# Local attention outputs of batches 3 to 7: probabilities as weights, and the rows turned by two DMA transposes a batch

## The chip, the cores and the metric

The kernel runs on one core of a Trainium2 chip. The metric is the device time of one execution in microseconds (us). A core has TensorE (PE, matrix multiplies, with its weight loads shown apart as PEld), VectorE (DVE), ScalarE (ACT), GpSimd (POOL) and SyncE (SP), each with an instruction queue of its own that is worked in order, and 16 DMA engines that all queues' transfers share. In this kernel SP asks for most transfers out of SBUF, and POOL for the loads, which turn f32 into bf16 on the way.

## The reference

Eight batches of causal sparse attention with eight heads (576 positions of 64) are followed by a feed-forward stage with a bilinear product. Heads 0 to 3 are local (a window of 32 positions), heads 4 to 7 strided (positions that agree modulo 32).

```python
scores = scale * np.matmul(q, k.transpose(0, 1, 3, 2))
rel = pos[:, None] - pos[None, :]
mask_local = (rel >= 0) & (rel < stride)
mask_strided = (rel >= 0) & (pos[None, :] % stride == pos[:, None] % stride)
scores = np.where(masks[None, :, :, :], scores, -1000000000.0)
attn = np.exp(scores - np.max(scores, axis=-1, keepdims=True))
attn = attn / (np.sum(attn, axis=-1, keepdims=True) + 1e-09)
attn_out = np.matmul(attn, v)
...
x = attn_out.transpose(0, 2, 1, 3).reshape(B * S, H * D)    # 4608 x 512
out = ((x @ w_a) * (x @ w_b)) @ w_out                        # d_ff = 1536
```

## The kernel before

**Two streams in one order.** The instruction order of each engine is written out by hand. The backbone is the feed-forward stage: nine tiles t of 512 tokens, each with 12 slots `ffn_ab` (f = 0 to 11; eight matmuls at L581, four with `wa_sb` and four with `wb_sb`, 512 tokens moving) and then four slots of the output product (`ffn_ys` at L669 for tiles 2 to 7, `ffn_y` at L733 for tiles 0 and 1; the last tile is written by `y_tail`). Slots are numbered through: 16 t + f. Attention is woven in: `take(i)` runs the steps of the table `LATER` for slot i and `IN_Y` for points within the output product. For batches b from 3 on, positions count from 16 (b - 1), so batch b is made during tile b - 1, and tile b needs it: `xT` holds the feed-forward's input with features on partitions, four chunks c of 128 features (c = 0 and 1 local heads, c = 2 and 3 strided heads) by a ring of 4 x 576 tokens. Tile t = b starts at token 512 b, batch b at token 576 b, and a matmul covers all 512 tokens of the tile (in tile 4 it is cut in two where the ring wraps). The first slot of a tile (f = 0) takes chunk 3 last, chunk 1 last in tile 1.

**A step S** (`S_p`, `S_x`, `S_m`) makes the scores of a unit u (chunk c = u // 2, half = u % 2), their exponentials (L392, ScalarE) and applies the mask in place (L402, VectorE). Keys lie on partitions, queries along the row: `p` is [keys, 2 heads, 288 queries]. Units 0 to 3 are local, with G = 3 blocks of 96 queries, and 4 to 7 strided, with 4 blocks of 72.

**A step V** makes the outputs of a unit. There are two forms:
- `step_VT` (batches 2 to 7): the values are the weights and p moves, 96 columns a block (L485, six matmuls for a local unit). The values' tile has columns of ones behind its 64 columns (`VW` = 128, set by `fill_v`), so the result `o` has 64 rows of outputs, already with features on partitions, and 64 rows of equal sums. The reciprocal is made on ScalarE as exp(-ln) (L494, L495, 64x576 each), and VectorE multiplies into `xT`, once for each head (L499 local, L501 strided).
- `V_p`, `V_r`, `V_n` (batches 0 and 1): p is the weights and the values move, 65 columns a block (64 and one of ones; L441). The result has queries on partitions; VectorE makes the reciprocals (L449) and multiplies into a row tile `xr` (L464). The steps X of TensorE (L510) then turn the rows, and ScalarE copies them into `xT` (L522).

Both forms have one PSUM buffer `o` from tile 0's end on.

**SP's queue.** A step D (`step_D`) transposes parts of q and k in 32x32 blocks on VectorE, and after the last part SP asks for the moves of the blocks into `kT` and `qz`: two moves for k's first pairs of heads, and ten after q's last part (L341, L345). In tile b - 1 the steps D of batch b + 1 run: its local k at slots 3 and 5, its local q at 7 and 9, its strided parts at 12 to 17. At one slot, `take` comes ahead of the steps D. `store_half` (L664) of the tile before is at slots 2 and 3. POOL's loads (L202, L211, L224, L242) each follow a `pace` instruction that reads something of their slot.

Of the kernel before, what the change touches and what calls it, by code (L numbers as in the profile page):

```python
# [8 lines left out]
BF16 = mybir.dt.bfloat16  # L9
# [5 lines left out]
FIRST_D = 2  # L15
RL = 6
RS = 8
# [4 lines left out]
LW = 96  # L22
# [8 lines left out]
def kernel(  # L31
# [10 lines left out]
    nc = tc.nc  # L42
    B, H, S, D = q.shape
# [9 lines left out]
    HL = H // 2  # L53
# [5 lines left out]
    sb = ctx.enter_context(tc.tile_pool(name="sb", bufs=3))  # L59
    fsb = ctx.enter_context(tc.tile_pool(name="ffn", bufs=2))  # L60
    pst = ctx.enter_context(tc.tile_pool(name="pst", bufs=1, space=bass.MemoryType.PSUM))
    dram = ctx.enter_context(tc.tile_pool(name="dram", bufs=2, space=bass.MemoryType.DRAM))
# [19 lines left out]
    vl_buf = [const.tile([128, HL * 6, VW], BF16, name=f"vl{i}") for i in range(2)]  # L82
# [30 lines left out]
    def zero_qz(i, eng, parts=((0, 0), (0, 1), (1, 0), (1, 1))):  # L113
        for j, z in parts:
            t = qz_buf[i][j][z]
            if (i, j, z) == (0, 0, 0):
                t = t[:, 1]
            if eng is nc.scalar:
                nc.scalar.copy(t, spare[:, :1].unsqueeze(2).to_broadcast(list(t.shape)))
            else:  # L120
                eng.memset(t, 0.0)
# [36 lines left out]
    XR = 4  # L158
    xT = const.tile([128, KD, XR * S], BF16)
# [11 lines left out]
    def fast_w(n, gs):  # L171
        a, b = ((wov[:, 0, 1], wov[:, 0, 0]), (wov[:, 1, 1], wf[:, 0]), (wov[:, 1, 1], wov[:, 0, 1]),
                (wov[:, 1, 0], wf[:, 1]))[n]
        nc.vector.tensor_tensor(wf[:, n, gs], a[:, gs], b[:, gs], op=ALU.subtract)
# [3 lines left out]
    def blocks(nm, z):  # L178
        z = int(z)
        return sb.tile([128, 2, (S, RS * GP)[z]], BF16, tag=f"t{nm}{z}", name=f"t{nm}{z}", bufs=1)  # L180
# [84 lines left out]
    def by_row(t):  # L265
        return t.rearrange("p (r h d) -> p h r d", h=2, d=D)

    def pair_up(nm, c):

        if (nm, c) == ("k", 1):  # L270
            t = shared[1][:96, -RL * 128:]
        else:
            t = blocks(*{"k0": "q0", "q0": "q1", "q1": "k0"}[f"{nm}{c}"])
            t = t.rearrange("p h n -> p (h n)")[:96, :RL * 128]
        nc.vector.tensor_copy(by_row(t), nats[1, nm, False][:, 2 * c:2 * c + 2])
        paired[1, nm, c] = t.rearrange("p (r m) -> p r m", r=RL)
# [85 lines left out]
    def unit(u):  # L362

        c, half = u // 2, u % 2
        return (c, half, 128, LW, 3) if c < 2 else (c, half, NP, NP, 4)
# [46 lines left out]
    xn = {}  # L412

    def V_p(b, u):
        c, half, M, n, G = unit(u)
        p = ps.pop((b, u))
        if b == 0:

            o = psum4["o"].tile([128, 512], F32, tag="o", name="o")
            if c < 2:  # L420
                of = o[:, :2 * G * (D + 1)].rearrange("p (j g e) -> p j g e", j=2, e=D + 1)
                sm = of[:, :, :, D:]
            else:
                of = o.rearrange("p (j g e) -> p j g e", j=2, e=D)
                sm = psum4["sum"].tile([128, 2, 4, 1], F32, tag="sum", name="sum")
        else:
            o = psum4["o"].tile([128, 2, 512], F32, tag="o", name="o")
            of = o[:, :, :G * (D + 1)].rearrange("p j (g e) -> p j g e", e=D + 1)
            sm = of[:, :, :, D:]
        for i in range(G):  # L430
            for j in range(2):
                if c < 2:
                    vt = vl_buf[b % 2][:, (2 * c + j) * 6 + 3 * half + i, 0:D + 1]
                elif b == 0:
                    r = 2 * i + j
                    vt = nats[0, "v", c - 2][:NP, half, r * D:(r + 1) * D]
                else:
                    vt = vs_buf[b % 2][:, 2 * (c - 2) + half, 2 * i + j, 0:D + 1]
                w = vt.shape[1]
                pt = p[:M, j, i * n:i * n + 128]  # L440
                nc.tensor.matmul(of[:, j, i, :w], lhsT=pt, rhs=vt, start=True, stop=True)  # L441
                if b == 0 and c >= 2:
                    nc.tensor.matmul(sm[:, j, i], lhsT=pt, rhs=vl_buf[0][:M, 0, D:D + 1], start=True, stop=True)
        held[b, "o", u] = of[:n, :, :, :D], sm[:n]

    def V_r(b, u):
        c, half, M, n, G = unit(u)
        rc = sb.tile([128, 2, 4], F32, tag="rc", name="rc")
        nc.vector.reciprocal(rc[:n, :, :G].unsqueeze(3), held[b, "o", u][1])  # L449
        held[b, "rc", u] = rc  # L450

    def V_n(b, u):
        c, half, M, n, G = unit(u)
        ov, _ = held.pop((b, "o", u))
        rc = held.pop((b, "rc", u))
        if (b, c // 2) not in xn:
            x = sb.tile([128, RS * 4 * D], BF16, tag="xr", name="xr", bufs=2)
            xn[b, c // 2] = x[:n, :S // n * 4 * D].rearrange("p (g h d) -> p g h d", h=4, d=D)
        x = xn[b, c // 2][:, :, 2 * (c % 2):2 * (c % 2) + 2, :]
        if c < 2 or b >= FIRST_D:  # L460
            dst = x[:, G * half:G * half + G].rearrange("p g j d -> p j g d")
        else:
            dst = x[:, :, half, :].rearrange("p (g j) d -> p j g d", j=2)
        nc.vector.tensor_mul(dst, ov, rc[:n, :, :G].unsqueeze(3).to_broadcast([n, 2, G, D]))  # L464

    def step_V(b, u):
        if b >= FIRST_D:
            step_VT(b, u)
            return
        V_p(b, u)  # L470
        V_r(b, u)
        V_n(b, u)

    def step_VT(b, u):

        c, half, M, n, G = unit(u)
        p = ps.pop((b, u))
        o = psum4["o"].tile([128, 2, 512], F32, tag="o", name="o")
        for i in range(G):
            for j in range(2):  # L480
                if c < 2:
                    vt = vl_buf[b % 2][:, (2 * c + j) * 6 + 3 * half + i]
                else:
                    vt = vs_buf[b % 2][:, 2 * (c - 2) + j, 4 * half + i]
                nc.tensor.matmul(o[:, j, i * n:(i + 1) * n], lhsT=vt, rhs=p[:M, j, i * n:(i + 1) * n], start=True, stop=True)  # L485

        r = sb.tile([128, RS * 4 * D], BF16, tag="xr", name="xr", bufs=2)[:64, :4 * W].bitcast(F32)
        r = r.rearrange("p (j w) -> p j w", j=2)
        if c < 2:
            sums = o[64:, :, :W]  # L490
        else:

            sums, r = (t.rearrange(e, p=NP) for t, e in ((o[64:, :, :W], "d j (g p) -> d j p g"), (r, "d j (p g) -> d j p g")))
        nc.scalar.activation(r, sums, ACT.Ln)  # L494
        nc.scalar.activation(r, r, ACT.Exp, scale=-1.0)  # L495
        for j in range(2):
            dst = xT[64 * j:64 * j + 64, c, S * (b % XR):S * (b % XR + 1)]
            if c < 2:
                nc.vector.tensor_mul(dst[:, W * half:W * (half + 1)], o[:64, j, :W], r[:, j])  # L499
            else:  # L500
                nc.vector.tensor_mul(dst.rearrange("d (p r) -> d p r", r=RS)[:, :, G * half:G * (half + 1)],  # L501
                                     o[:64, j, :W].rearrange("d (g p) -> d p g", p=NP), r[:, j])
# [21 lines left out]
    def step_X(b, c):  # L524
# [20 lines left out]
    LATER = {-1: "S0", 0: "S1", 1: "V0", 2: "S2", 3: "V1", 4: "S3", 5: "V2", 6: "S4", 7: "V3", 8: "S5", 9: "V4", 10: "S6",  # L545
             11: "V5"}
    IN_Y = {2: "S7", 6: "V6", 11: "V7"}
    FN = {"Tk": step_Tk, "Tq": step_Tq, "S": step_S, "V": step_V, "X": step_X, "W": lambda b, n: fast_w(n, slice(0, 3)),
          "s": S_px, "m": S_m, "L": lead_vl, "Pk": lambda b, c: pair_up("k", c), "Pq": lambda b, c: pair_up("q", c),
          "Z": lambda b, n: zero_qz(0, nc.vector, ((1, 1),)), "D": lambda b, n: step_D(FIRST_D, 0, "k", n)}  # L550

    def run(b, slot):
# [209 lines left out]
    with tc.manual_schedule(engines={ENG.PE, ENG.SP, ENG.Pool, ENG.DVE, ENG.Activation}):  # L762
# [11 lines left out]
        for x, src in ((raw[0], k), (raw[1], q)):  # L774
            nc.sync.dma_start(out=x[:96].rearrange("p (h r d) -> p h r d", h=2, d=D),
                              in_=src[0, 0:2].rearrange("h (p r) d -> p h r d", r=RL))
# [62 lines left out]
        for b in range(1, B):  # L839
            for pos, names in (STEPS.get(b) or {16 * (b - 1) + x: n for x, n in LATER.items()}).items():  # L840
                steps.setdefault(pos, []).append((b, names.split()))
# [6 lines left out]
        def do(i, fn, *args):  # L848
            at.setdefault(i, []).append(lambda: fn(*args))
# [34 lines left out]
        for i, jz in ((2, (0, 0)), (3, (1, 0)), (0, (0, 1))):  # L884
            do(i, zero_qz, 0, nc.vector, (jz,))
        do(14, rezero, 1)
        do(27, fill_v, vl_buf[1])
        do(28, fill_v, vs_buf[1])
        for n, slot in enumerate((16, 16, 19, 20)):
            do(slot, fast_w, n, slice(3, 6))  # L890
# [50 lines left out]
```

## Time and profile before

| what | before |
|---|---|
| median of 3 runs | 328.92 us (328.76 to 329.47) |
| profiled execution, whole | 329.03 us |
| its span, in which the profile counts | 327.3 us |
| tiles 2, 3, 4, 5, 6 of the feed-forward stage, about | 34.0, 34.0, 34.6, 34.0, 33.8 us |
| share of the chain of waits: L581 / L669 / L733 | 54% / 17% / 6% |
| share of the chain of waits: L485 / L441 | 4% / 1% |
| granted TensorE clock, mean | 0.998 |

A tile is about 34 us, and an `ffn_ab` slot without attention work in it about 1.73 us of TensorE. The chain of waits goes back from the last instruction to what released each, so its shares add to the span; busy times of engines overlap and don't. In the lists of groups, the number ahead of the second bar is the mean of one instruction in ns; what stands behind that bar is idle time of the engine ahead of the group. In the order of time, an engine's lines give start, length and the group; matmuls follow each other closer than their length, so two starts tell the distance.

### The profile page before, as it was taken

What the parts mean: (1) busy time and instruction counts of PE and PEld (TensorE: products, weight loads), DVE (VectorE), ACT (ScalarE), POOL (GpSimd) and SP (SyncE); (2) the same over time, 40 slices, a digit from 0 to 9 for tenths busy, and PEclk for the clock granted to TensorE, in tenths of its full rate; (3) what the DMA queues carried; (4) which work ended last, traced back from release to release, by engine and by line L of the source; (5) the groups of instructions that cost most, each with busy time, mean ns of one, the idle gap of its engine ahead of it and who ended that gap; (6) DMA issues with size and microseconds to landing.
All of it is one profiled execution on the core that took longest, in us unless ns stands there. A gap on an engine that the chain in (4) does not pass through costs nothing.

```text
span 327.3 us, 7626 instructions
## 1 busy us (share of the span) xinstructions
PE 319.6 (98%) x2788; PEld 205.5 (63%) x2820; DVE 250.6 (77%) x529; ACT 210.1 (64%) x345; POOL 151.6 (46%) x280
## 2 busy tenths in 40 slices
PE   8999999999999999999999999999999999999994
PEld 6754555455555587557999885569555954584474
DVE  6766788888778989799879988998878745626652
ACT  6763775478777776777677767876777743323341
POOL 8935948599966554664475346644011001100000
PEclk9999999999999999999999999999999999999999
DMA  9999999999999699999899969897033040004004
GB/s 154 151 203 201 202 184 174 174 173 127 140 213 120 87 95 84 98 222 100 80 85 199 127 69 99 175 159 84 20 78 114 2 131 0 0 2 129 0 2 128
DMA packets 98725, 37.50 MB, mean 115 GB/s; under 512 B 76672, under 2 KB 95744, under 8 KB 98688
## 3 DMA queue, kind: packets, MB, share of 16 engines
q0 software_dynamic: 85968, 19.48, 64.4%
q1 hardware_dynamic: 12576, 17.47, 18.3%
q8 instruction: 22, 0.36, 0.4%
q14 instruction: 15, 0.12, 0.1%
q10 hardware_dynamic: 144, 0.07, 0.1%
HBM read 39.51 MB, written 9.44 MB: 150 GB/s over the span
## 4 chain that ended last, share of the span: by engine, by line
PE 90%; POOL 3%; DMA 3%; DVE 1%; issue 1%; ACT 0%; POOLq 0%
PE mm L581 54%; PE mm L669 17%; PE mm L733 6%; PE st L384 4%; PE o L485 4%; DMA wb_sb<-in_moe_w_b_dram 3%; PE mm L698 2%; POOL shared L196 1%; PE end L698 1%; POOL vl L224 1%; PE o L441 1%; POOL wa_sb L251 0%; POOL tk L237 0%; PE tp L286 0%; PE tp L295 0%
## 5 line engine op out<-in xcount | busy, mean ns | idle before, releaser
L581 PE MATMUL mm<-xT,wb_sb 128*128 128x512 bf16 (+1 forms) x465 | 109.1, 357 | 0.3
L581 PE MATMUL mm<-xT,wa_sb 128*128 128x512 bf16 (+1 forms) x451 | 107.7, 356 | 1.1
L598 ACT COPY a_sb<-mm 128x512 f32<-128x512 f32 x106 | 62.1, 586 | 45.7 <-PE mm L581 45.0
L907 POOL CAST pace<-pf 1x1 f32<-1x1 bf16 x87 | 24.6, 283 | 113.0 <-DVE pf L601 109.8
L581 PEld LDWEIGHTS <-wb_sb 128*128 128x128 bf16 x480 | 46.2, 98 | 44.7 <-DMA wb_sb<-in_moe_w_b_dram 1.1
L601 DVE TENSOR_TENSOR pf<-a_sb,mm 128x512 bf16<-128x512 f32 x84 | 57.0, 679 | 18.5 <-PE mm L581 14.2
L581 PEld LDWEIGHTS <-wa_sb 128*128 128x128 bf16 x480 | 42.7, 98 | 31.3
L494 ACT ACTIVATE xr<-o 64x576 f32<-64x576 f32 x48 | 31.1, 648 | 22.8 <-PE o L485 22.5
L392 ACT ACTIVATE p<-st 128x576 bf16<-128x576 f32 (+1 forms) x64 | 41.6, 650 | 6.3 <-PE st L384 5.7
L495 ACT ACTIVATE xr<-xr 64x576 f32<-64x576 f32 x48 | 32.8, 683 | 1.5
L499 DVE TENSOR_TENSOR xT<-o,xr 64x288 bf16<-64x288 f32 x48 | 21.6, 449 | 13.5 <-ACT xr L495 13.0
L501 DVE TENSOR_TENSOR xT<-o,xr 64x288 bf16<-64x288 f32 x48 | 21.4, 446 | 11.8 <-ACT xr L495 11.2
L669 PEld LDWEIGHTS <-ps 128*128 128x128 bf16 x288 | 27.9, 98 | 3.1
L646 ACT COPY y_sb<-mm 128x512 f32<-128x512 f32 (+1 forms) x28 | 15.6, 556 | 17.9 <-PE mm L669 13.0
L669 PE MATMUL mm<-wf,ps 128*128 128x256 bf16 x216 | 25.6, 273 | 0.0
L733 PE MATMUL mm<-wo_sb,pf 128*128 128x512 bf16 x93 | 22.9, 379 | 0.1
L242 POOL DMA_DIRECT2D vs<-in_v_dram x24 | 19.7, 820 | 5.0 <-PE mm L669 2.4
L669 PEld LDWEIGHTS <-pf 128*128 128x128 bf16 x216 | 20.3, 98 | 2.5 <-issue 0.2
L669 PE MATMUL mm<-wo_sb,pf 128*128 128x256 bf16 x144 | 18.5, 273 | 0.1
L603 DVE TENSOR_TENSOR pf<-a_sb,mm 128x512 bf16<-128x512 f32 x22 | 14.9, 677 | 4.7 <-ACT a_sb L598 2.6
L211 POOL DMA_DIRECT2D ql<-in_q_dram x24 | 16.0, 666 | 5.0 <-DMA wo_sb<-in_moe_w_out_dram 3.9
L211 POOL DMA_DIRECT2D kl<-in_k_dram x24 | 16.0, 667 | 4.8 <-issue 4.0
(152 smaller groups left out, 471.6 us busy)
## 6 DMA issues: line engine op xcount, KB each, us to landing
out_dram<-y_sb SPq DMA_DIRECT2D x12, 512.0 KB, 4.9
out_dram<-y_sb SPq DMA_DIRECT2D x11, 256.0 KB, 3.8
vl<-in_v_dram POOLq DMA_DIRECT2D x6, 384.0 KB, 6.8
kl<-in_k_dram POOLq DMA_DIRECT2D x24, 72.0 KB, 3.4
ql<-in_q_dram POOLq DMA_DIRECT2D x24, 72.0 KB, 3.3
vs<-in_v_dram POOLq DMA_DIRECT2D x24, 72.0 KB, 3.7
wo_sb<-in_moe_w_out_dram POOLq DMA_DIRECT2D x4, 384.0 KB, 9.0
natk<-in_k_dram POOLq DMA_DIRECT2D x20, 72.0 KB, 3.3
```

The lines of the kernel that those rows point to most:

```text
L211: nc.gpsimd.dma_start(out=t[32 * h:32 * h + 32], in_=src[b, h].rearrange("(i y) d -> y i d", y=32))
L392: nc.scalar.activation(p[:M, :, :W], st[:M, :, :W], ACT.Exp, scale=scale)
L494: nc.scalar.activation(r, sums, ACT.Ln)
L495: nc.scalar.activation(r, r, ACT.Exp, scale=-1.0)
L499: nc.vector.tensor_mul(dst[:, W * half:W * (half + 1)], o[:64, j, :W], r[:, j])
L501: nc.vector.tensor_mul(dst.rearrange("d (p r) -> d p r", r=RS)[:, :, G * half:G * (half + 1)], o[:64, j, :W].rearrange("d (g p) -> d p g", ...
L581: nc.tensor.matmul(ps_[:, c0:c0 + n], lhsT=w[:, kk, 128 * f:128 * (f + 1)], rhs=xT[:, kk, x0:x0 + n], start=(kk == first and c0 == 0), sto ...
L598: nc.scalar.copy(a_sb, ab[0])
L601: nc.vector.tensor_mul(pf[:, f, :].rearrange("p (i a s) -> p a i s", i=2, s=16), halves(a_sb), halves(ab[1]))
L669: nc.tensor.matmul(bank[b][:, q], lhsT=lhs(g, q), rhs=rhs(g), start=k in "172" and q == 0 and g == 0, stop=g == FG - 1, skip_group_check=True)
L733: nc.tensor.matmul(ybank[j], lhsT=pf[:, f, 128 * j:128 * (j + 1)], rhs=wo_sb[:, f], start=(f == 0), stop=(f == FD - 1))
L907: nc.gpsimd.tensor_copy(pace, done)
```

## The change

For batches 3 to 7 the local units (u = 0 to 3) take the second form: `step_V` goes to `step_VT` only for strided units and for batch 2. The rows of a batch's four local units are gathered in a tile `xl` (96 queries of a block on partitions, 6 blocks, 256 features). After V3, at slot 7, a new step O asks SP to write them to a buffer in DRAM (576 rows of 256 features; two buffers in turn). At slot 10 a new step I asks SP, for chunk 0 and for chunk 1, for a DMA transpose of 128 features of all 576 rows into `xT`. The steps D at slot 9 come before it, so on SP's queue the write stands between the moves of slot 5 and those of slot 9, and the two transposes behind the ten moves of slot 9 and ahead of those of slot 14. For batch 7, which has no steps D in its tile, the transposes directly follow the write. The steps X are not used for these rows. The fill of the ones in the second local values' buffer (`vl_buf[1]`, at slot 27) falls away; the column that the sums need is set elsewhere (L104).

```diff
@@ V_n
         if (b, c // 2) not in xn:
-            x = sb.tile([128, RS * 4 * D], BF16, tag="xr", name="xr", bufs=2)
+            if b >= FIRST_D:
+                x = sb.tile([128, RL * 4 * D], BF16, tag="xl", name="xl", bufs=1)
+            else:
+                x = sb.tile([128, RS * 4 * D], BF16, tag="xr", name="xr", bufs=2)
...
     def step_V(b, u):
-        if b >= FIRST_D:
+        if b >= FIRST_D and (u >= 4 or b == FIRST_D):
             step_VT(b, u)
             return
...
+    scratch = {}
+
+    def rows_out(b, _):
+
+        scratch[b] = dram.tile([S, HL * D], BF16, tag="xd", name="xd")
+        nc.sync.dma_start(out=scratch[b].rearrange("(g p) e -> p g e", p=LW),
+                          in_=xn.pop((b, 0)).rearrange("p g h d -> p g (h d)"))
+
+    def rows_in(b, c):
+
+        nc.sync.dma_start(out=xT[:, c, S * (b % XR):S * (b % XR + 1)], in_=scratch[b][:, 128 * c:128 * (c + 1)],
+                          transpose=True)
...
     LATER = {-1: "S0", 0: "S1", 1: "V0", 2: "S2", 3: "V1", 4: "S3", 5: "V2", 6: "S4",
-             7: "V3", 8: "S5", 9: "V4", 10: "S6", 11: "V5"}
+             7: "V3 O0", 8: "S5", 9: "V4", 10: "S6 I0 I1", 11: "V5"}
...
+          "O": rows_out, "I": rows_in,
...
-        do(27, fill_v, vl_buf[1])
```

More of the change, by code (lines that the diff above doesn't have):

```diff
@@ L544 @@
                  27.5: "V4", 28: "S6", 28.5: "V5", 29: "S7", 29.5: "V6", 30.5: "V7"}}
-    LATER = {-1: "S0", 0: "S1", 1: "V0", 2: "S2", 3: "V1", 4: "S3", 5: "V2", 6: "S4", 7: "V3", 8: "S5", 9: "V4", 10: "S6",
+    LATER = {-1: "S0", 0: "S1", 1: "V0", 2: "S2", 3: "V1", 4: "S3", 5: "V2", 6: "S4", 7: "V3 O0", 8: "S5", 9: "V4", 10: "S6 I0 I1",
              11: "V5"}
@@ L548 @@
     FN = {"Tk": step_Tk, "Tq": step_Tq, "S": step_S, "V": step_V, "X": step_X, "W": lambda b, n: fast_w(n, slice(0, 3)),
-          "s": S_px, "m": S_m, "L": lead_vl, "Pk": lambda b, c: pair_up("k", c), "Pq": lambda b, c: pair_up("q", c),
+          "s": S_px, "m": S_m, "L": lead_vl, "O": rows_out, "I": rows_in, "Pk": lambda b, c: pair_up("k", c), "Pq": lambda b, c: pair_up("q", c),
           "Z": lambda b, n: zero_qz(0, nc.vector, ((1, 1),)), "D": lambda b, n: step_D(FIRST_D, 0, "k", n)}
```

## The prediction

> **What bounds the kernel now.** I read the page's busy shares first, then its chain of waits, then the stages, then the order of time on TensorE and on SP's queue around one tile boundary.
>
> ```profile
> span 327.3 us, 7626 instructions
> PE 319.6 (98%) x2788; PEld 205.5 (63%) x2820; DVE 250.6 (77%) x529; ACT 210.1 (64%) x345; POOL 151.6 (46%) x280
> PE 90%; POOL 3%; DMA 3%; DVE 1%; issue 1%; ACT 0%; POOLq 0%
> ```
>
> TensorE is on 90% of the chain. Since matmuls overlap, busy time alone proves little, so I look at when each group starts:
>
> ```profile
> 53.69 0.35 PE L441 MATMUL o<-vl,p 128*128 128x65 bf16 x6
> 53.88 0.42 PE L510 MATMUL tp<-ident,xr 96*128 96x96 bf16 x6
> ...
> 207.03 0.42 PE L485 MATMUL o<-p,vl 128*128 128x96 bf16 x6
> 207.28 1.03 PE L581 MATMUL mm<-xT,wa_sb 128*128 128x512 bf16 x4
> ```
>
> The first column is a group's start. The next group starts 0.25 us after an old local unit (L485, 96 columns moving) and 0.19 us after a unit of the new form, which batch 1 already runs (L441, 65 columns; the other free-standing ones give 0.19 and 0.18). TensorE's whole list of waits holds 1.5 us, all before 57 us. So from 93 to 263 us, where batches 3 to 7 are made, TensorE sets the time: what it is spared comes off, and what it is made to wait comes on.
>
> Then the end of tile 5 (its outputs of batch 6 are read by tile 6), on SP's queue and on TensorE:
>
> ```profile
> 218.57 0.55 SPq L345 DMA_DIRECT2D qz10l<-tq  x1
> ...
> 224.25 0.59 SPq L345 DMA_DIRECT2D qz11l<-tq  x1
> 229.16 1.14 SPq L341 DMA_DIRECT2D kT1s<-tk  x2
> ```
> ```profile
> 229.38 0.21 PE L384 MATMUL st<-qz11l,kT1l 128*128 128x96 bf16 x1
> 229.63 0.59 PE L581 MATMUL mm<-xT,wa_sb 128*128 128x512 bf16 x2
> ```
>
> Ten moves keep SP's queue from 218.57 to 224.84 (some 0.63 apart), and the next tile's first L581 is due at 229.42 (the six L384 start 0.042 apart; of the eight first L581 one record is missing). That is the room for what is asked for behind the moves.
>
> **The change, part by part.**
>
> *TensorE.* 20 units (4 local units in each of 5 batches) go from 0.25 to 0.185 us: 20 x 0.065 = 1.3 us saved. Bounds: by columns alone, 6 x (96 - 65) x (0.25/576) = 0.081 a unit, 1.6 in all; nothing, if loading the masked weights p were no longer covered. I take 1.3, since batch 1's row has this very instruction with this very weight load. The weights now wait for the mask on VectorE, but S runs two or three slots ahead of its V, and each slot is 2 us.
>
> *ScalarE and VectorE.*
>
> ```profile
> L494 ACT ACTIVATE xr<-o 64x576 f32<-64x576 f32 x48 | 31.1, 648 | 22.8 <-PE o L485 22.5
> L495 ACT ACTIVATE xr<-xr 64x576 f32<-64x576 f32 x48 | 32.8, 683 | 1.5
> L499 DVE TENSOR_TENSOR xT<-o,xr 64x288 bf16<-64x288 f32 x48 | 21.6, 449 | 13.5 <-ACT xr L495 13.0
> L464 DVE TENSOR_TENSOR xr<-o,rc 96x384 bf16<-96x384 f32 x8 | 4.3, 547 | 0.2
> L449 DVE RECIPROCAL rc<-o 96x6 f32<-96x6 f32 x8 | 1.5, 188 | 2.4 <-PE o L441 2.2
> ```
>
> The shares behind the second bar are idle time. A unit drops L494 and L495 (1.331 us of ScalarE, 26.6 in all) and changes two L499 (0.898) for L449 and L464 (0.735): 3.3 us less VectorE. Both lie beside TensorE, so I cost them at nothing. The single o bank is freed sooner. One stall on VectorE stands in the chain, at tile 4's first output matmul (185.18, some 0.5 us late), but it follows strided unit V4 and its exponentials, which stay; it is a bound below (-0.5). The dropped fill of vl (1.4 us of POOL) is beside everything too.
>
> *SP's queue: three issues a batch.* Rows out: V3 is at slot 7, and in tile 5 its last VectorE instruction ends near 213.6 (it takes the place of the L499 of 212.84, 0.735 long). SP is then held by two k moves until 214.31, so it writes from 214.3 to 214.9, and the q moves behind it, which VectorE lets go at 218.57, are not delayed. The nearest writes to DRAM (256 to 512 KB) land in 3.8 to 4.9 us, so these 288 KB are there by 219.8, before the queue is free at 224.84. No cost. Then the two transposes, 576 rows of 256 bytes each. Behind them stand the strided k moves, which VectorE lets go at 229.16; their scores are at slot 6 of the next tile, some 13 us later, and can bear it.
>
> *The new wait.* The tile's first matmul needs x chunk 0 and its second chunk 1 (only chunk 3 is taken late). By the same two views the room from SP free to need is, for chunk 1: tile 2, 122.76 to 127.2, 4.45 us; tile 3, 156.30 to 161.36, 5.06 (its cut comes between); tile 4, 190.91 to 195.80, 4.87; tile 5, 4.79. Chunk 0 has 0.2 less. For batch 7 there are no q moves in tile 6 and the transposes go out at slot 10 after the write lands, with some 13 us: no stall. Behind a waiting first matmul stands all of TensorE, so a stall is paid in full, four times.
>
> No transpose is in this trace. Bounds of one from issue to landing:
>
> ```profile
> DMA to landing us min/median/max: 1.8/1.9/4.2
> DMA to landing us min/median/max: 3.0/3.6/5.2
> DMA to landing us min/median/max: 6.2/6.8/6.9
> ```
>
> First the 36 KB moves into qz10l, then the 72 KB loads of vs, then the 384 KB loads of vl, all between 93 and 263 us. Below: 1.9, and chunk 1 is there at 0.6 + 1.9 = 2.5: no stall. Above: 6.8 each, one behind the other, 13.6. A vs load has as many pieces (72 x 8 = 576 rows) as a transpose has, each half as long; so I take its slowest, 5.2, with 0.6 for the issue of the first: chunk 1 lands 5.8 after SP is free. Stalls: 1.35 + 0.74 + 0.93 + 1.01 = 4.0 us. The four vs loads themselves are under way then (220.17 to 225.0 in tile 5), sharing the engines, so the short end is unlikely.
>
> The Trainium skill has two figures that point opposite ways, and no row here shows either. "DMA: Bandwidth & Descriptors", Latency and other measured facts, gives a DMA transpose 261 GB/s: estimated 0.56 us for 147 KB, which would leave no stall and 327.6. "VectorE: DVE Perf Modes", The three transpose paths, has 1309 ns for 128x128 by DMA against 390 by TensorE, and advises TensorE where PSUM is a fit target, so it speaks against this change: 4.5 such blocks are an estimated 5.9 us, two in a row 11.8, some 28 us of stalls and about 356.
>
> **Sum.** 327.3 - 1.3 + 4.0 = 330.0 of span. The profiled execution took 329.03, 1.7 more than its span, and the median of the runs shown is 328.92; against that, 328.92 + 2.7 = 331.6.
>
> **Rivals.**
>
> *The transposes fit the room.* Then only the saving is left: 328.92 - 1.3 = 327.6, down to 327.1 with tile 4's 0.5. For it: SP's plain moves land in 1.9 to 3.4 (medians) in the same stretch, and the DMA share is at most 0.03 in the 2 us around the ends of tiles 2 to 4. Against: the second transpose is issued 4 us before its need and the loads of vs are in the way. It decides as long as chunk 1 lands within 4.9 us of SP being free (stalls 0.45 + 0.03 + 0.11 = 0.6).
>
> *The two serialize at the price of a vl load.* Chunk 1 at 13.6: stalls 9.15 + 8.54 + 8.73 + 8.81 = 35.2, so 328.9 - 1.3 + 35.2 = 362.8. For it: an unknown cutting into pieces. Against: a vl load has 3072 pieces.
>
> *Saving and stalls cancel.* Chunk 1 between 4.9 and 5.3 (stalls 0.6 to 2.0): 328.3 to 329.6. That the change does not do what it says (p's weight loads uncovered) would add 1.3 to any case; I give it next to nothing beside batch 1's 0.185.
>
> **Chances.** Forecast, a late chunk 1 with 329.6 to 342 (landing 5.3 to 8.4): 0.45. It fits: 0.36. Cancelled: 0.10. Serialized, beyond 342: 0.09. About 0.2% (0.66 us) is what a measurement of this kernel can tell from no change; so faster 0.36, same 0.10, slower 0.45 + 0.09 = 0.54. The range runs from 327.1 to 342, and the forecast's own from 329.6.
>
> **What would show it.** Right: L441 groups of six 0.19 us apart in tiles 2 to 6; ScalarE's busy time near 183; and at the start of tiles 3 to 6, not of 7, a wait of TensorE on a DMA into xT, longest in tile 3, with landings of 5 to 6 us. Wrong: no such wait (the first rival), waits near 9 us (the second), transposes that hold SP past 231 so that strided moves are late, or a wait at V's weights for the mask.

## The result and the profile after

| what | before | after |
|---|---|---|
| median of 20 runs each, side by side | 329.22 us | 331.95 us |
| ratio to before, with its 95% interval | | 1.0079 [1.0061, 1.0098] |
| span of the profiled execution | 327.3 us | 330.1 us |
| TensorE's waits for a DMA into `xT` | none | 3.4 us in 4 (4.04 by start times, see below) |
| ScalarE / VectorE / POOL busy | 210.1 / 250.6 / 151.6 us | 183.5 / 247.6 / 148.9 us |

The kernel became slower by 0.8%. In the changed kernel the lines have moved: L581 is now L597, L669 is L685, L485 is L501, L494 and L495 are L510 and L511, L464 is L467; the rows' write is L482 and the transposes are L487.

The page after, its first lines and the shares of its chain of waits:

```profile
span 330.1 us, 7618 instructions
PE 321.0 (97%) x2820; PEld 204.4 (62%) x2820; DVE 247.6 (75%) x529; ACT 183.5 (56%) x305; POOL 148.9 (45%) x279
PE 71%; DMA 12%; SPq 8%; POOL 4%; DVE 2%; issue 1%; ACT 1%; POOLq 0%
```

TensorE's share of the chain fell from 90% to 71%, and DMA and SP's queue now hold 20% of it. That does not mean that 19% of the time was lost. The chain follows the last releaser: where TensorE waits a microsecond for a transfer, the chain goes back through the whole transfer, its issue and the moves ahead of it on SP, while TensorE was computing during nearly all of that. The loss is read from the waits and from start times instead. TensorE's list of waits (us in total, times, longest) has at its head:

```profile
PE mm L597 <- DMA xT<-xd: 3.4, 4, 1.1
```

Four waits, one at the start of each of tiles 3 to 6, and none in tile 7. Here is the first, as the order of time shows it on SP's queue (SPq: SP asking for transfers), and then on TensorE (start, length, group; in brackets the idle time before it and what ended it):

```profile
122.21 0.59 SPq L345 DMA_DIRECT2D qz01l<-tq  x1
122.85 2.59 SPq L487 DMA_TRANSPOSE xT<-xd  x2
126.38 1.15 SPq L341 DMA_DIRECT2D kT0s<-tk  x2
```
```profile
126.60 0.21 PE L384 MATMUL st<-qz01l,kT0l 128*128 128x96 bf16 x1
126.64 0.38 PE L597 MATMUL mm<-xT,wa_sb 128*128 128x512 bf16 x1
127.96 0.59 PE L597 MATMUL mm<-xT,wa_sb 128*128 128x512 bf16 x2 [0.94 <-DMA xT<-xd]
```

The first L597 of the tile (chunk 0) runs on time at 126.64. The second (chunk 1) is due 0.22 later, at 126.86, and starts at 127.96: 1.10 us lost. The bracket says 0.94, since it counts from the modelled end of the matmul before. The chain in order of time (start, length, piece) says what was late:

```profile
122.85 1.28 SPq L487
124.13 0.05 issue
124.18 3.74 DMA xT<-xd
127.92 0.04 issue
127.96 1.67 PE mm L597 x7
```

One transpose holds SP's queue for 1.28 us. The second, asked for at 124.18, is in place 3.74 later, so chunk 1 lands 5.07 after SP was free. The transposes' line over all ten (shortest, median and longest hold of the queue in ns), and their time from issue to landing:

```profile
L487 SPq DMA_TRANSPOSE xT<-xd x10: 1154/1262/1284, 122.8 to 253.5; - x10
DMA to landing us min/median/max: 2.5/3.5/4.8
```

The same reading at the four tile starts (room: from SP being free to the first matmul that needs the new part of chunk 1):

| start of tile | chunk 1 lands after SP is free | room | lost by start times |
|---|---|---|---|
| 3 | 5.07 | 4.01 | 1.10 |
| 4 | 6.12 | 4.86 | 1.30 |
| 5 | 5.69 | 4.44 | 1.29 |
| 6 | 4.13 | 3.83 | 0.35 |
| sum | | | 4.04 |

The gain is there too. A free-standing local unit in tile 2, and the groups with one shape each:

```profile
96.61 0.34 PE L441 MATMUL o<-vl,p 128*128 128x65 bf16 x6
96.79 1.03 PE L597 MATMUL mm<-xT,wa_sb 128*128 128x512 bf16 x4
```
```profile
L441 PE MATMUL o<-vl,p 128*128 128x65 bf16 x168 | 9.5, 193 | 0.0
L467 DVE TENSOR_TENSOR xl<-o,rc 96x384 bf16<-96x384 f32 x20 | 11.1, 553 | 0.7
```

The next group starts 0.18 us after the unit, where an old unit took 0.25, and 168 matmuls of this form had no idle time ahead of them: the weight load of the masked p is covered. From the first scores of tile 2 to the first output matmul of tile 7, before took 191.34 us (92.57 to 283.91) and after 193.95 (92.65 to 286.60), so 2.61 of the 2.8 us of span lie between these two points, which take in the five tiles that the change touches.

### The profile page after: what moved, and what is told of

It reads as the page before. It is cut to its first block, busy times and chain, and to the rows that moved or that the text cites. A ratio compares the mean times of both kernels' runs of the same rounds, so it can differ in the third digit from the quotient of the medians.

```text
span 330.1 us, 7618 instructions
## 1 busy us (share of the span) xinstructions
PE 321.0 (97%) x2820; PEld 204.4 (62%) x2820; DVE 247.6 (75%) x529; ACT 183.5 (56%) x305; POOL 148.9 (45%) x279
## 4 chain that ended last, share of the span: by engine, by line
PE 71%; DMA 12%; SPq 8%; POOL 4%; DVE 2%; issue 1%; ACT 1%; POOLq 0%
PE mm L597 48%; DMA wb_sb<-in_moe_w_b_dram 7%; PE mm L685 6%; PE mm L749 6%; SPq L345 5%; DMA xT<-xd 5%; PE st L384 3%; PE mm L714 2%; PE o L441 2%; SPq L487 2%; PE o L501 1%; SPq L341 1%; POOL shared L196 1%; PE end L714 1%; DVE xT L517 1%
## 5 line engine op out<-in xcount | busy, mean ns | idle before, releaser
L597 PE MATMUL mm<-xT,wa_sb 128*128 128x512 bf16 (+1 forms) x472 | 111.0, 357 | 3.4 <-DMA xT<-xd 3.4
L597 PE MATMUL mm<-xT,wb_sb 128*128 128x512 bf16 (+1 forms) x472 | 110.3, 357 | 0.1
L614 ACT COPY a_sb<-mm 128x512 f32<-128x512 f32 x106 | 62.1, 586 | 75.6 <-PE mm L597 74.3
L922 POOL CAST pace<-pf 1x1 f32<-1x1 bf16 x87 | 22.7, 261 | 113.5 <-DVE pf L617 97.6
L597 PEld LDWEIGHTS <-wb_sb 128*128 128x128 bf16 x480 | 46.2, 98 | 44.6 <-DMA wb_sb<-in_moe_w_b_dram 0.8
L597 PEld LDWEIGHTS <-wa_sb 128*128 128x128 bf16 x480 | 42.3, 98 | 35.4 <-issue 4.4
L517 DVE TENSOR_TENSOR xT<-o,xr 64x288 bf16<-64x288 f32 x48 | 21.4, 446 | 15.5 <-ACT xr L511 15.0
L685 PEld LDWEIGHTS <-ps 128*128 128x128 bf16 x288 | 27.8, 98 | 3.2
L685 PE MATMUL mm<-wf,ps 128*128 128x256 bf16 x216 | 25.6, 273 | 0.0
L662 ACT COPY y_sb<-mm 128x512 f32<-128x512 f32 (+1 forms) x28 | 15.6, 556 | 17.9 <-PE mm L685 13.8
L510 ACT ACTIVATE xr<-o 64x576 f32<-64x576 f32 x28 | 18.1, 648 | 12.0 <-PE o L501 11.6
L685 PEld LDWEIGHTS <-pf 128*128 128x128 bf16 x216 | 20.2, 98 | 2.6 <-issue 0.2
L511 ACT ACTIVATE xr<-xr 64x576 f32<-64x576 f32 x28 | 19.1, 683 | 0.9
L685 PE MATMUL mm<-wo_sb,pf 128*128 128x256 bf16 x144 | 18.5, 273 | 0.1
L631 DVE TENSOR_TENSOR ps<-pf 128x512 bf16<-128x512 bf16 (+1 forms) x48 | 17.7, 380 | 0.4
```

Of the source, the lines that this page charges most:

```text
L597: nc.tensor.matmul(ps_[:, c0:c0 + n], lhsT=w[:, kk, 128 * f:128 * (f + 1)], rhs=xT[:, kk, x0:x0 + n], start=(kk == first and c0 == 0), sto ...
L614: nc.scalar.copy(a_sb, ab[0])
L685: nc.tensor.matmul(bank[b][:, q], lhsT=lhs(g, q), rhs=rhs(g), start=k in "172" and q == 0 and g == 0, stop=g == FG - 1, skip_group_check=True)
L922: nc.gpsimd.tensor_copy(pace, done)
```

## The experiments

Each ratio is to the kernel before, run beside it on the same chip. Diffs are against the changed kernel.

**The transposes ahead of the q moves.** Tests whether the place on SP's queue is the whole loss. Only the slot of step I changes, from 10 to 9, where `take` comes ahead of the q moves.

```diff
-    LATER = {-1: "S0", 0: "S1", 1: "V0", 2: "S2", 3: "V1", 4: "S3", 5: "V2", 6: "S4", 7: "V3 O0", 8: "S5", 9: "V4", 10: "S6 I0 I1",
-             11: "V5"}
+    LATER = {-1: "S0", 0: "S1", 1: "V0", 2: "S2", 3: "V1", 4: "S3", 5: "V2", 6: "S4", 7: "V3 O0", 8: "S5", 9: "V4 I0 I1", 10: "S6",
+             11: "V5"}
```

> The two transposes of a batch are asked for at slot 9 ahead of that slot's ten q moves, right behind the write of the rows. Theory (the loss is TensorE waiting at the starts of tiles 3 to 6 for chunk 1, 4.0 us in all, against 1.3 us saved by the shorter matmuls): chunk 1 lands some 5 us before its need, the four waits go, and only the saving is left: ratio to the kernel before 0.996, some 327.8 us. The q moves start up to 1.4 us later, with 4 us to spare before their scores. Rival (the extra transfers or the new form of V cost time wherever they stand, by sharing engines and queues): as the changed kernel, 1.006 to 1.010.

Measured: 328.22 us against 328.94, 0.9993 [0.9973, 1.0013], span 326.1. The order of time on SP, and TensorE at the start of tile 3:

```profile
112.92 2.51 SPq L487 DMA_TRANSPOSE xT<-xd  x2
115.86 0.55 SPq L345 DMA_DIRECT2D qz00l<-tq  x1
```
```profile
126.67 0.21 PE L384 MATMUL st<-qz01l,kT0l 128*128 128x96 bf16 x1
126.71 0.59 PE L597 MATMUL mm<-xT,wa_sb 128*128 128x512 bf16 x2
```

In tile 2 the transposes go out 10 us earlier and are through before VectorE lets the q moves go, and the first two L597 of tile 3 run as one group without a gap. In tiles 3 to 5 the order has a price on SP: its list of waits holds 20.0 us, in five waits over the whole execution, for the rows' write to land ahead of the transposes. The q moves behind them start 26.6, 27.2 and 26.6 us after the tile's first scores, where before they started at 23.4, 23.6 and 23.4; that is more than the 1.4 us expected, and still TensorE waits for none of them. The tiles' starts are now 33.74, 34.24 and 33.73 us apart for tiles 3, 4 and 5, against 34.03, 34.52 and 34.02 before: 0.29 less in each, which is the pure saving of four units. From tile 2's first scores to tile 7's first outputs it is 189.90 us, 1.44 less than before. So the loss hangs on the place in the queue; the transposes themselves cost TensorE nothing that shows.

**Chunk 1 taken later.** Tests whether the tile's first matmuls wait for chunk 1 alone. The transposes stay behind the moves; the first slot of tiles 3 and on takes chunk 2 first, then 0, then 1.

```diff
-                ab_mm(t, f, ab, [kk for kk in range(KD) if kk != late], last=-1)
+                if t >= 3:
+                    ab_mm(t, f, ab, [2], first=2, last=-1)
+                    ab_mm(t, f, ab, [0], first=-1, last=-1)
+                    ab_mm(t, f, ab, [1], first=-1, last=-1)
+                else:
+                    ab_mm(t, f, ab, [kk for kk in range(KD) if kk != late], last=-1)
```

> Everything as in the changed kernel, but the first slot of tiles 3 to 8 takes its chunks in the order 2, 0, 1, 3, each for both weights, so chunk 1 is needed three matmuls (0.65 us) later. Theory: of the waits of 1.10, 1.30, 1.29 and 0.35 us the first three shrink by 0.65 and the last goes: 2.3 us back, some 329.6 us, ratio 1.001. Rival (extra transfers cost time wherever they stand): no change, 1.008.

Measured: 329.71 against 328.94, 1.0026 [1.0006, 1.0045], span 327.3. The list of waits keeps one of 0.3 us. By start times more is left: from a tile's first scores to the first local unit it is 4.31, 4.00, 4.42 and 4.18 us in tiles 3 to 6, where the experiment above has 3.97, 4.01, 3.96 and 3.97. That is 1.0 in all, and 1.44 - 1.0 is what this kernel spares in tiles 2 to 7 (190.92 us against 191.34, so 0.42). Chunk 1 is now the fifth matmul and not the second, 0.65 us later, and chunk 0 the third. The rest is seen at tile 5:

```profile
195.87 0.38 PE L597 MATMUL mm<-xT,wb_sb 128*128 128x512 bf16 x1
196.55 0.38 PE L597 MATMUL mm<-xT,wa_sb 128*128 128x512 bf16 x1 [0.30 <-DMA xT<-xd]
```

Two matmuls that follow each other stand 0.22 apart; here it is 0.68, so chunk 1 was still 0.46 late. Of the 1.0, chunk 1 has 0.6 (tiles 3 and 5) and chunk 0 has 0.4 (tiles 3 and 6). About three quarters of the 4.04 us came back through the order of four matmuls: the loss is the time at which chunk 1 is needed, not work that was added.

**Plain copies in place of the transposes.** Tests whether it is the transposing that is slow, or any DMA in this place. The same 144 KB for each chunk go from the DRAM buffer into the same part of `xT`, at the same point of SP's queue. What is computed differs: chunks 0 and 1 of batches 3 to 7 hold the rows unturned.

```diff
-        nc.sync.dma_start(out=xT[:, c, S * (b % XR):S * (b % XR + 1)], in_=scratch[b][:, 128 * c:128 * (c + 1)],
-                          transpose=True)
+        flat = scratch[b].rearrange("s e -> (s e)").rearrange("(c p f) -> c p f", c=2, p=128)
+        nc.sync.dma_start(out=xT[:, c, S * (b % XR):S * (b % XR + 1)], in_=flat[c])
```

> The two transposes stay where they are, behind the ten moves, but are plain copies of the same 144 KB each, so chunks 0 and 1 of batches 3 to 7 are not turned. If it is the transpose's own price (1.26 us of SP for each and 2.8 to 4.8 us more to landing for the second): a plain issue is 0.6 and lands in about 3.5, chunk 1 at 4.1 after SP is free, inside every tile's room: ratio 0.996 to 0.998, some 328. If the place behind the moves is enough by itself, whatever the kind of transfer: waits near those of the changed kernel, above 1.005.

Measured: 328.16 against 328.94, 0.9973 [0.9939, 1.0008], span 325.5, no wait on `xT`. SP's order of time at the same point:

```profile
122.29 1.06 SPq L488 DMA_DIRECT2D xT<-xd  x2
```

Two plain copies hold the queue for 1.06 us together where two transposes held it for 2.59, and they land in 3.3 us in the median where a transpose takes 3.5. So the transfers themselves are hardly longer. What makes chunk 1 late is mainly the first transpose's hold on the queue, 1.28 instead of 0.53, and the long cases of the landing (4.8 at most, against 3.9). Taking the 0.75 us of the longer hold off each of the four losses in the table above would leave 0.35 + 0.55 + 0.54 + 0, so 1.4 of the 4.04 us (an estimate from these rows).

**The transposes done, but read by nobody.** Tests contention: the kernel before, with the write and the two transposes added at the changed kernel's places on SP's queue, from and into tiles that nothing else uses.

```diff
     def step_V(b, u):
-        if b >= FIRST_D and (u >= 4 or b == FIRST_D):
+        if b >= FIRST_D:
             step_VT(b, u)
...
-        nc.sync.dma_start(out=scratch[b].rearrange("(g p) e -> p g e", p=LW),
-                          in_=xn.pop((b, 0)).rearrange("p g h d -> p g (h d)"))
+        nc.sync.dma_start(out=scratch[b].rearrange("(g p) e -> p g e", p=LW), in_=spare_x)
...
-        nc.sync.dma_start(out=xT[:, c, S * (b % XR):S * (b % XR + 1)], in_=scratch[b][:, 128 * c:128 * (c + 1)],
-                          transpose=True)
+        nc.sync.dma_start(out=spare_t[:, c], in_=scratch[b][:, 128 * c:128 * (c + 1)], transpose=True)
...
+        do(27, fill_v, vl_buf[1])
```

> The kernel before with all outputs made in the old form, and in addition the write of the rows (from a constant tile) and the two transposes of each batch at the same places, into a tile that nothing reads. Theory: nobody waits, and SP and the DMA engines have room: within 0.4 us of the kernel before, ratio 0.999 to 1.002. Rival (extra transfers cost time by sharing engines and queues): it carries the larger part of the loss, 1.005 or more.

Measured: 329.23 against 328.94, 1.0001 [0.9971, 1.0031], span 327.5. Tiles 3, 4 and 5 take 34.03, 34.52 and 34.02 us, to the hundredth those of before. The ten transposes and five writes, with the same landings (2.6 to 4.8), delay neither moves nor loads so that TensorE would feel it. The cost that is left is the wait of the matmul that reads them.

**The transposes on ScalarE's queue.** Tests whether another queue, with the idle time that ScalarE has gained, can issue them in time.

```diff
-        nc.sync.dma_start(out=xT[:, c, S * (b % XR):S * (b % XR + 1)], in_=scratch[b][:, 128 * c:128 * (c + 1)],
+        nc.scalar.dma_start(out=xT[:, c, S * (b % XR):S * (b % XR + 1)], in_=scratch[b][:, 128 * c:128 * (c + 1)],
                           transpose=True)
```

> As the changed kernel, but the two transposes of a batch are asked for on ScalarE's queue, at the same slot 10, so they stand behind no moves. Theory: the waits of tiles 3 to 6 on DMAs into xT go, since the transposes start some 6 us earlier; but each holds the queue that issues it for 1.26 us, here ahead of the copies of slot 11 (L614), so those are some 2.5 us late in five tiles. If the four PSUM banks of the slots cover that: 327.7 us, ratio 0.996; if not, up to 1 us a tile back, to 332. Rival (transposes are slow wherever they are asked for): the waits on xT stay.

Measured: 341.63 against 328.86, 1.0343 [1.0302, 1.0384], span 339.5: much slower than either theory had it. ScalarE's order of time in tile 3, and the head of TensorE's waits:

```profile
148.12 0.65 ACT L392 ACTIVATE p<-st 72x576 bf16<-72x576 f32 x1
152.05 2.69 ACTq L487 DMA_TRANSPOSE xT<-xd  x2
154.83 0.59 ACT L614 COPY a_sb<-mm 128x512 f32<-128x512 f32 x1 [6.07 <-issue]
```
```profile
PE mm L685 <- ACT y_sb L662: 10.3, 5, 4.2
```

No matmul waits for `xT` any more. But the transposes wait at the head of ScalarE's queue for the rows' write to land (asked for at 144.86, in place 7.2 us later), and then hold the queue for 2.69 us: ScalarE makes nothing from 148.77 to 154.83. What is queued behind is the copy L614 of the slot's result, and later the copies L662 that free TensorE's output banks. On SP, which computes nothing, the same wait added no time to a tile in the first experiment. The wait was moved to a queue with work behind it.

**The vs loads four slots later.** Tests the prediction's picture that the four loads of vs, under way at the same time, stretch the transposes' landing.

```diff
-                    do(g0 + h + 10, load_vs, b, (h,))
+                    do(g0 + h + 14, load_vs, b, (h,))
```

> As the changed kernel with its order on SP, but POOL's four loads of the strided values stand four slots later (14 to 17 of the tile instead of 10 to 13), so they are not under way with the transposes. If sharing the DMA engines with them makes the second transpose's landing 2.8 to 4.8 us: it falls to the 2.5 us that batch 7's had with quiet engines, chunk 1 is there 2 x 1.27 + 2.5 = 3.8 to 4.0 us after SP is free (from the first transpose's start), inside every tile's room, and the ratio is 0.996 to 0.998. If a transpose's landing is its own, the waits stay: 1.006 to 1.010.

Measured: 331.1 against 328.86, 1.0063 [1.0042, 1.0084]; the expected gain did not come. TensorE's wait on `xT` still sums to 3.6 us in three. The chain in order of time at the start of tile 3:

```profile
124.60 1.28 SPq L487
125.88 0.05 issue
125.93 3.06 DMA xT<-xd
128.99 0.04 issue
129.03 0.38 PE mm L597
```

Here chunk 1 lands 4.4 us after SP is free, 0.7 sooner than in the changed kernel, but in the next tile it still took 5.8, and the q moves moved too (some 1.1 us later against the tile's start), which ate what was gained. The experiment is not clean for this reason. In its trace the first transposes of tiles 2 to 5 landed in 2.9, 2.7, 2.7 and 3.0 us, where the changed kernel's took 3.5, 3.8, 3.3 and 3.5; but the second ones, for which TensorE waits, took 3.1, 4.5, 4.6 and 3.0, against 3.7, 4.8, 4.4 and 2.8. So the vs loads are not what makes the second landing long; why it is 2.8 in one tile and 4.8 in another stays open.

**The transposes ahead, and batch 2 in the new form as well.** Four more local units would spare another 0.29 us. `LATER` is as in the first experiment.

```diff
-        if b >= FIRST_D and (u >= 4 or b == FIRST_D):
+        if b >= FIRST_D and u >= 4:
...
-             2: {20: "S0", 20.5: "S1", 21.5: "V0", 22: "S2", 23: "V1", 23.5: "S3", 24.5: "V2", 25: "S4", 26: "V3", 26.5: "S5",
-                 27.5: "V4", 28: "S6", 28.5: "V5", 29: "S7", 29.5: "V6", 30.5: "V7"}}
+             2: {20: "S0", 20.5: "S1", 21.5: "V0", 22: "S2", 23: "V1", 23.5: "S3", 24.5: "V2", 25: "S4", 26: "V3 O0", 26.5: "S5",
+                 27: "I0 I1", 27.5: "V4", 28: "S6", 28.5: "V5", 29: "S7", 29.5: "V6", 30.5: "V7"}}
...
...
-        do(0, fill_v, vl_buf[0])
```

> The transposes ahead of the moves as in e1_ahead, and batch 2's local units in the new form too (write at slot 26, transposes at slot 27, ahead of that slot's moves; the fill of the first values' buffer falls away). Theory: four more units at 0.08 us less each and no wait: 0.3 us below e1_ahead, 1.6 + 0.3 = 1.9 us below the kernel before, ratio 0.994. Rival: tile 2 starts with a wait for batch 2's chunk 1, and the ratio is that of e1_ahead or above.

Measured: 329.3 against 328.86, 1.003 [1.0004, 1.0057], span 326.8. It missed. In its list of waits stands a new one at the start of tile 2, and the chain in order of time leads to it:

```profile
PE st L384 <- DMA qz11l<-tq: 1.2, 1, 1.2
```
```profile
89.73 0.58 SPq L345
90.36 2.93 DMA qz11l<-tq
93.33 0.20 PE st L384
```

In tile 1 the queue has no such room, and it is the q moves of batch 3, now later on SP, that the scores wait for. The lateness went to the other transfer of the same queue.

**The first experiment twice more, and with the dropped fill.** The trace showed 1.44 us spared and the medians 0.7. The second kernel of each pair also puts the fill of `vl_buf[1]` back, the one part of the change that lies ahead of tile 2.

```diff
+        do(27, fill_v, vl_buf[1])
```

> The same kernel as e1_ahead, beside e7_ahead_batch2 on the same chip. With the saving measured between the starts of tiles 2 and 7 there (168.71 against 170.37 us): 1.6 us below the kernel before, ratio 0.995; if those 1.6 us are given back before tile 2 or after tile 7: 0.998 or above.

> e1_ahead with the fill of ones at slot 27 put back on POOL, which nothing needs. In the traces e1_ahead spares 1.4 us between the first matmul of tile 2 and the first output matmul of tile 7, but its medians lie only 0.7 to 0.8 us below the kernel before. If the missing fill moves loads on POOL ahead of tile 2 and costs the difference: some 0.6 us below e1_ahead, ratio 0.995 to 0.996. If it is a cost of another kind or chance: as e1_ahead, 0.998.

> e1_ahead beside e12_ahead_fill on one chip, to settle whether the fill at slot 27 is worth the difference between their medians in separate comparisons (328.0 and 328.2 for e1_ahead's, 327.5 with the fill): ratio 0.997 to 0.998 if the fill matters, the same as e12_ahead_fill if the difference was chance.

> e1_ahead with the fill at slot 27 put back, beside e11_ahead. If the fill matters: 0.5 us or more below e11_ahead, ratio 0.995. If the difference was chance: equal to it within 0.3 us.

| kernel | median | before | ratio | span |
|---|---|---|---|---|
| ahead, again | 328.03 | 328.86 | 0.9980 [0.9962, 0.9998] | 326.3 |
| ahead, with the fill | 327.53 | 329.15 | 0.9978 [0.9950, 1.0006] | 325.3 |
| ahead, third time | 327.83 | 328.98 | 0.9972 [0.9946, 0.9997] | 325.9 |
| ahead, with the fill, beside the third | 328.32 | 328.98 | 0.9976 [0.9952, 1.0001] | 326.7 |

The fill makes no difference that can be told: side by side, the kernel with it was 0.5 us slower in the median with overlapping intervals, and against before the two stand at 0.9976 and 0.9972. The version with the transposes ahead stands at 0.9993, 0.9980 and 0.9972 in its three comparisons, and two of the three intervals lie below 1; the 0.995 to 0.996 expected of the first two was not reached. Its medians lie 0.7 to 1.2 us below those of the kernel before. Why the medians show up to 0.7 less than the trace's 1.44 is open: the first scores of tile 2, with nothing but the fill changed ahead of them, start between 91.90 and 93.34 us in the profiled executions of these five kernels (the two ends are the two with the fill), so the load phase alone scatters by as much as is looked for.

**The transposes behind the k moves.** Makes the suspected wait several times as long: step I stands at slot 15, behind the strided k moves.

```diff
-    LATER = {-1: "S0", 0: "S1", 1: "V0", 2: "S2", 3: "V1", 4: "S3", 5: "V2", 6: "S4", 7: "V3 O0", 8: "S5", 9: "V4", 10: "S6 I0 I1",
-             11: "V5"}
+    LATER = {-1: "S0", 0: "S1", 1: "V0", 2: "S2", 3: "V1", 4: "S3", 5: "V2", 6: "S4", 7: "V3 O0", 8: "S5", 9: "V4", 10: "S6",
+             11: "V5", 15: "I0 I1"}
```

> The changed kernel with the transposes asked for at slot 15, behind the two strided k moves as well, which end on SP 4.7 us after the transposes' place there. Theory (chunk 1's lateness is paid by TensorE in full, in tiles 3 to 6): the waits grow from 1.10, 1.30, 1.29 and 0.35 to 5.8, 6.7, 6.4 and 4.8 us, 19.7 more in all: some 351 us, ratio 1.067; batch 7 has no moves and stays without a wait. Rival (lateness is partly hidden by the other engines catching up, or the loss has another source): below 1.05.

Measured: 358.77 against 329.15, 1.0902 [1.0877, 1.0927], span 354.5. The waits on `xT` sum to 21.3 us, near what was expected of them, but the kernel is 28.4 us longer than the one with the transposes ahead (354.5 - 326.1), and not 21. The windows around the first wait (stretch, length, busy time and count of PE, PEld, DVE, ACT, POOL, then granted clock, DMA share, GB/s), and TensorE's order of time there:

```profile
128.00:129.00 1.00, 0.00 (x0) 0.00 (x0) 0.54 (x1) 0.00 (x0) 0.70 (x2) 1.00 1.57 170
129.00:130.00 1.00, 0.00 (x0) 0.00 (x0) 0.00 (x0) 0.00 (x0) 0.00 (x0) 0.59 1.70 125
...
135.00:136.00 1.00, 1.00 (x3) 0.29 (x2) 0.00 (x0) 0.15 (x1) 0.00 (x0) 0.50 0.00 0
136.00:137.00 1.00, 1.00 (x11) 0.63 (x10) 0.54 (x1) 0.96 (x2) 0.00 (x0) 1.00 0.00 0
```
```profile
126.19 0.21 PE L384 MATMUL st<-qz01l,kT0l 128*128 128x96 bf16 x1
132.49 1.61 PE L597 MATMUL mm<-xT,wa_sb 128*128 128x512 bf16 x3 [6.09 <-DMA xT<-xd]
```

TensorE stops at 126.40. The granted clock falls to 0.50 within the window from 129 to 130, some 2.8 us into the wait, and is back only in the window from 136, 3.5 us after the matmuls have started again. The tile's first eight matmuls in that stretch stand 0.44 us apart in the mean and not 0.22: 8 x 0.22 = 1.8 us more. At the other three tile starts (waits of 5.4 and 5.2 us, and of 3.6 and 1.0 with one matmul between them) the clock is at 0.50 for 3.4 us as well, and the matmuls behind the wait take 1.7, 1.6 and 1.7 us longer. That makes 6.7 of the 28.4 - 21.3 = 7.1 us, so the slow matmuls account for nearly all of the difference.

## Why the prediction was right

Its main line held: SP's queue hands the transposes over too late, TensorE pays the lateness in full four times, and a small saving stands against it. By its steps:

- **TensorE's saving.** Predicted 1.3 (0.065 a unit), between 0 and 1.6. Where no wait covers it, 0.29 us a tile of four units were measured, 0.072 a unit, 1.44 for the twenty. The weight load of masked p is covered, as batch 1's row had it; the truth lies between that row and the bound by columns (0.081).
- **ScalarE, VectorE, POOL.** ScalarE was predicted near 183 and took 183.5; VectorE was to have 3.3 less and has 3.0. All of it lies beside TensorE, as costed; TensorE's list of waits has none on them but 0.3 us at 15 us, far ahead of the changed tiles.
- **The rows' write.** Predicted at no cost, landing 3.8 to 4.9 us after its issue. Those two figures are the medians of the 256 KB and the 512 KB writes over the whole execution and not the bounds of single ones; between 140 and 245 us the 512 KB writes of before took 4.1 to 6.9. The rows' write lands in 4.6 in the median (2.7 to 6.2), before SP comes to the transposes in tiles 2 to 5, so the step holds with these figures too, and the idle transposes show the same tile times as before.
- **Contention.** Costed at nothing, and the idle transposes confirm it at 1.0001. The other half of that picture, that the loads of vs stretch the landing, fits the first transpose of a pair (with these loads moved away it took 2.7 to 3.0 us and not 3.3 to 3.8) but not the second, which sets the wait.
- **Chunk 1's landing.** Predicted 5.8 in every tile, as 0.6 for the issue of the first and 5.2 for the second. Measured 5.07, 6.12, 5.69 and 4.13, from about 1.33 (hold of the queue and the gap) and 3.7, 4.8, 4.4 and 2.8. The terms were off against each other: no row of before showed that a transpose holds its queue for twice as long as a plain move, and the slowest load of vs was too high a price for all four landings.
- **The room.** Predicted 4.45, 5.06, 4.87 and 4.79; it was 4.01, 4.86, 4.44 and 3.83. The first three were misread by some 0.15 to 0.19: the order of time of before puts chunk 1's first use at 127.06, 161.20 and 195.61, not 127.2, 161.36 and 195.80 (and the third difference was written 4.87 for 4.89). Read rightly, the rooms of before are 4.30, 4.90, 4.70 and 4.79. What is then missing (0.29, 0.04, 0.26 and 0.96) is mostly the time for which the ten moves keep SP's queue, from the start of the first to the end of the last: 7.00, 6.28, 6.88 and 7.19 us, where before it was 6.76, 6.27, 6.66 and 6.27. Single moves held the queue for 1.16 to 1.34 us and not 0.59, and the last one of tile 5 also started 0.35 late. Why is open. The saving did not shorten the room: beside the waits at the tiles' starts, the first q move starts 0.27 to 0.30 us earlier after the tile's first scores, as TensorE does at its end. The prediction took the holds of one execution as fixed.
- **Their sum.** Stalls of 1.35 + 0.74 + 0.93 + 1.01 = 4.0 were predicted, 1.10 + 1.30 + 1.29 + 0.35 = 4.04 measured. That the sum is right to 0.1 is luck: no single tile is right to better than 0.2, and over the four the landings came 2.2 us sooner and the rooms were 2.0 shorter. With the rooms of before read rightly the same landing would have given 4.5. In the changed kernel chunk 0 was never waited for, and batch 7 not at all, as said.
- **The rivals.** The transposes did not fit the room, and the plain copies show by how little: with 0.5 us of issue and not 1.3 they did. They did not cost what a vl load costs; the longest landing was 4.8, not 6.8. Saving and stalls did not cancel in the changed kernel; with chunk 1 put off they nearly did, with 0.42 us spared in the tiles and a ratio of 1.0026.

The room in lines: the first three are before's, with chunk 1 first used at the start of the first and the third (chunk 0's record is missing) and, as the fourth matmul of half the length, 0.33 us into the second. Then come the first q move of tile 2 in before, and, in the changed kernel, that move and a long one.

```profile
127.06 0.59 PE L581 MATMUL mm<-xT,wa_sb 128*128 128x512 bf16 x2
160.87 0.82 PE L581 MATMUL mm<-xT,wa_sb 128*128 128x256 bf16 x6
195.61 0.59 PE L581 MATMUL mm<-xT,wa_sb 128*128 128x512 bf16 x2
```
```profile
116.00 0.54 SPq L345 DMA_DIRECT2D qz00l<-tq  x1
```
```profile
115.80 0.54 SPq L345 DMA_DIRECT2D qz00l<-tq  x1
117.65 1.34 SPq L345 DMA_DIRECT2D qz01l<-tq  x1
```

The span grew by 2.8 where 2.7 was predicted, and the medians by 2.73. Of the two figures of the Trainium skill that the prediction set against each other, neither gave the landing: the 0.56 us worked out from the bandwidth ("DMA: Bandwidth & Descriptors", Latency and other measured facts) is far below the 2.5 us of the fastest, and the 5.9 us worked out by blocks ("VectorE: DVE Perf Modes", The three transpose paths) is above the slowest, 4.8.

## What to carry to other kernels

Where a transfer is asked for behind others on a queue, its landing counts from when the queue is free and includes how long each issue ahead of it holds the queue; where it can be had early, put it ahead of what is not yet needed, and look at what that pushes back. Take the room from several tiles and leave a margin: the same ten moves kept the queue for 6.3 to 7.2 us here. A queue of an engine that computes is no free place for a transfer that still has to wait for its data.

## What the hardware showed that was not expected

- A DMA transpose of 576 rows by 128 features held SP's queue for 1.15 to 1.28 us in the changed kernel (single ones of the other kernels for up to 2.56, with medians of 1.23 to 1.27), and ScalarE's for 1.15 to 1.39. A plain copy of the same 144 KB held SP's for 0.33 to 1.05, with a median of 0.44.
- A long wait costs more than itself. Waits of up to 1.3 us left the granted clock at 1.00. The four of 4.6 to 6.1 us behind the k moves brought it to 0.50, which cost 1.6 to 1.8 us more each. By the windows it fell at 129.18, 173.54, 214.51 and 255.46 (2.8, 5.2, 4.8 and 5.1 us after TensorE stopped, in the last case with one matmul in between) and came back at 136.00, 176.96, 217.92 and 258.88: all eight changes lie whole multiples of 3.41 us apart. The Trainium skill ("TensorE: Matmul & The Clock Gate", Part 1) puts the change to half rate, and the return from it, at one window of about 3.4 us, running freely. The spacing here agrees. The 3.41 us that end with the first fall begin at 125.77, while TensorE worked until 126.40: such a window need not be idle from its start.
- Landings of equal transposes varied from 2.5 to 4.8 us in the changed kernel. With the loads of vs taken away the second of a pair still varied from 3.0 to 4.6 in tiles 2 to 5, and the cause was not found.
